# A fused scan and feed-forward kernel: 512 tokens a matmul instead of 256 from token 1024 on

## The chip, the cores and the metric

The kernel runs on one core of a Trainium2 chip. The metric is device time in microseconds; a lower number is better. A run's time is that of the core; "span" is the time from the first to the last instruction in the profiled execution.

## What is computed

```python
batch, n_heads, seq, head_dim, d_state = 4, 8, 768, 32, 16      # x, a, B, C
n_tokens, d_model, d_ff = 3072, 256, 2048                       # w_in, w_out

# a state-space scan, per batch and head (the reference goes in chunks of 32; any chunk gives the same)
L = exp(cum[i] - cum[j]) for i >= j, else 0          # cum: running sum of log(a) in the chunk
y = ((C @ B.T) * L) @ x + (C @ state) * exp(cum)
state = exp(sum(log a)) * state + B.T @ (x * exp(cum[-1] - cum))

# then a feed-forward layer on the 3072 tokens, 8 heads x 32 = 256 features
h = y @ w_in
g = h - tanh(h)
out = g @ w_out
```

All inputs are fp32 but the weights, which are fp64 and are converted on the chip into two fp32r parts (wh, wl).

## The kernel before

**Scan.** Each of the 4 sequences is cut into 7 chunks of 112 tokens (the last has 96), 28 chunks in all. A chunk has two parts on TensorE. `chunk_a` makes the decay exponents and C times B in one `att` tile (matmuls at L452 and L458); ScalarE takes the exponential (L462), VectorE multiplies (L466), GpSimd zeroes the upper triangle (L469). `chunk_y` makes y (L494) and the next state (L502) in a `y` tile in PSUM; ScalarE copies the state in four pieces to the next chunk's operand (L507) and y's high part to `xh` (L514), and VectorE subtracts to get the low part `xl` (L519). So the feed-forward input is held as two fp32r parts, high and low, one pair of tiles a sequence, two sequences at a time.

**Feed-forward.** The 2048 hidden features are 16 blocks of 128, taken in 8 pairs `u`. The tokens are 12 tiles `t` of 256. A step is one (t, u). `mm1` (L545) forms the hidden values of a tile and a pair of blocks in one PSUM bank `ph` (128 x 2 x 256): for each block, 6 matmuls of 256 columns (wh and wl with xh, wh with xl, each over two halves of the 256 features). `act` then does the tanh on ScalarE (L559), the subtraction on VectorE (L563), the high part `gh` on ScalarE (L567) and the low part `gl` on VectorE (L574). `mm2` (L595) adds the step's part of the output to one PSUM bank `po` (128 x 2 x 256): 12 matmuls of 256 columns. Each matmul has a weight load of its own.

PSUM: two banks `ph`, one `po`, one `y`, four for `att`.

**Order of the work.** The weights arrive and are converted (`load_w`, `conv`) while the first work runs, so the first four tiles (tokens 0 to 1023) go in four sweeps, each over two pairs `u`, and their output sums are kept in `pt` between sweeps (`keep`, L609 and L616). The eight tiles behind them go through all eight pairs at once. At its last pair a tile's sum is copied, on ScalarE and VectorE a half each (L629, L631; with `pt` added at L627 in the first four tiles), to `ob` and stored by two DMAs on SyncE's queue (`store`, L634). `mm2` is entered two steps (`LAG`) behind `mm1`. The chunks that a tile needs are spread over the steps of the tile ahead of it.

The order on each engine is not written by hand. Each operation is entered with its engine, a cost in us, what it reads and what it writes; `slot` names the buffers of a ring, and a buffer is free for its next use when the earlier readers are done. `Order.plan` simulates that list with priorities, in 16 rounds with random jitter and then 1500 random tries on the first 110 us, and keeps the best. The instructions are issued in the order of the simulated starts.

Of the kernel before, what the change touches and what calls it, by code (L numbers as in the profile page):

```python
# [31 lines left out]
NT = T // TT  # L32
# [12 lines left out]
SWEEPS = 0, 2, 4, 6, 8  # L45


class Order:
# [24 lines left out]
    def __call__(self, eng, cost, fn, r=(), w=(), dma=0, after=()):  # L73
# [134 lines left out]
def tile_ssm_moe(ctx: ExitStack, tc: tile.TileContext, a, x, bn, bc, wts, out):  # L208
# [16 lines left out]

    chunks, ends = {}, 0
    for t in range(NT):
        b, j = divmod(t, S // TT)
        end = b * CPB + -(-(j + 1) * TT // Q)
        chunks[t], ends = list(range(ends, end)), end  # L230
# [4 lines left out]
    SPAN = slice(len(chunks[0]), len(chunks[0]) + 7), slice(len(chunks[0]) + 7, NCK)  # L235
# [49 lines left out]
    wl = cp.tile([P, NCONV, 2, 2, 256], F32R, name="wl")  # L285

# [85 lines left out]
    def first_tile():  # L372
# [39 lines left out]
        for ck in range(len(chunks[0])):  # L412
# [65 lines left out]
    def chunk_y(ck):  # L478
# [4 lines left out]
        n_y = slot("y", 1)  # L483
# [6 lines left out]
        def fn():  # L490
            y = k["y"] = ps_y.tile([P, 2 * H * D], F32, tag="y", name=f"y{ck}")
# [17 lines left out]

        def fn_h():  # L510
            if c == 0:
                seq[b]["xh"] = p3.tile([P, 2, S], F32R, tag="xh", name=f"xh{b}", bufs=2)
            k["yv"] = k["y"][:, 0 : 2 * Q].rearrange("p (g q) -> p g q", g=2)[:, :, 0:q]
            nc.scalar.copy(seq[b]["xh"][:, :, c * Q : c * Q + q], k["yv"])  # L514

        def fn_l():
            if c == 0:
                seq[b]["xl"] = p3.tile([P, 2, S], F32R, tag="xl", name=f"xl{b}", bufs=2)
            nc.vector.tensor_tensor(out=seq[b]["xl"][:, :, c * Q : c * Q + q], in0=k["yv"],  # L519
                                    in1=seq[b]["xh"][:, :, c * Q : c * Q + q].bitcast(F32), op=ALU.subtract)  # L520
# [9 lines left out]
    def mm1(t, u):  # L530
        b, j = divmod(t, S // TT)
        d, ts = seq[b], slice(j * TT, (j + 1) * TT)
        cs = [c for c in range(CPB) if c * Q < ts.stop and (c + 1) * Q > ts.start]
        n_h, n_g = slot("ph", NPH), slot("g", 3)
        gs[t, u, 0] = [n_h, n_g]

        def fn():
            ph = ps_h.tile([P, 2, TT], F32, tag="ph", name=f"ph{t}_{u}")
            gs[t, u] = [ph]
            for j in range(2):  # L540

                for p in range(2):
                    for k in range(2):
                        for w_ in (wh, wl)[: 2 - p]:
                            nc.tensor.matmul(out=ph[:, j, :], lhsT=w_[:, u, 0, k, j * P : (j + 1) * P],  # L545
                                             rhs=d[("xh", "xl")[p]][:, k, ts], start=p == 0 and k == 0 and w_ is wh,
                                             stop=p == 1 and k == 1, skip_group_check=True)

        op("PE", 1.41, fn, r=[*[d["n_xh"][c] for c in cs], *[d["n_xl"][c] for c in cs], f"wh{u}.0", f"wl{u}.0"], w=[n_h])

    def act(t, u, eng):
        n_h, n_g = gs[t, u, 0]
        n_gh, n_gl = slot("gh", 3), slot("gl", 3)
        gs[t, u, 0] += [n_gh, n_gl]

        def fn_t():
            g = p3.tile([P, 2, TT], F32, tag="g", name=f"g{t}_{u}")
            gs[t, u].append(g)
            nc.scalar.activation(g, gs[t, u][0], AF.Tanh)  # L559

        def fn_s():
            ph, g = gs[t, u]
            nc.vector.tensor_tensor(out=g, in0=ph, in1=g, op=ALU.subtract)  # L563

        def fn_h():
            gh = p3.tile([P, 2, TT], F32R, tag="gh", name=f"gh{t}_{u}")
            nc.scalar.copy(gh, gs[t, u][1])  # L567
            gs[t, u].append(gh)

        def fn_l():  # L570
            _, g, gh = gs[t, u]
            gl = p3.tile([P, 2, TT], F32R, tag="gl", name=f"gl{t}_{u}")
            on = nc.vector if eng == "DVE" else nc.gpsimd
            on.tensor_tensor(out=gl, in0=g, in1=gh.bitcast(F32), op=ALU.subtract)  # L574
            gs[t, u].append(gl)
# [4 lines left out]
        op(eng, 0.8 if eng == "DVE" else 1.8, fn_l, r=[n_g, n_gh], w=[n_gl])  # L580

    def mm2(t, u, seg):

        _, _, n_h, n_l = gs[t, u, 0]
        if u == seg[0]:
            n_po[t, seg] = slot("po", 1)

        def fn():
            _, _, gh, gl = gs[t, u]
            if u == seg[0]:  # L590
                po[t, seg] = ps_o.tile([P, 2, TT], F32, tag="po", name=f"o{t}_{u}")
            for k, (w_, g) in enumerate(((wh, gh), (wl, gh), (wh, gl))):
                for j in range(2):
                    for e in range(2):
                        nc.tensor.matmul(out=po[t, seg][:, e, :], lhsT=w_[:, u, 1, j, e * P : (e + 1) * P],  # L595
                                         rhs=g[:, j, :], start=u == seg[0] and k == 0 and j == 0 and e == 0,
                                         stop=u == seg[-1] and k == 2 and j == 1, skip_group_check=True)

        op("PE", 1.41, fn, r=[n_h, n_l, f"wh{u}.1", f"wl{u}.1"], w=[n_po[t, seg]])
        if u == seg[-1]:  # L600
            if u < NCONV - 1:
                keep(t, seg)
            else:
                store(t, seg)

    def keep(t, seg):

        if seg[0]:
            op("DVE", 0.69, lambda: nc.vector.tensor_tensor(out=pts[t], in0=po[t, seg], in1=pts[t], op=ALU.add),  # L609
               r=[n_po[t, seg]], w=[n_pt[t]])  # L610
            return
        n_pt[t] = slot("pt", NSW)

        def fn():
            pts[t] = p1.tile([P, 2, TT], F32, tag="pt", name=f"pt{t}", bufs=NSW)
            nc.scalar.copy(pts[t], po[t, seg])  # L616

        op("ACT", 0.6, fn, r=[n_po[t, seg]], w=[n_pt[t]])

    def store(t, seg):  # L620
        name = op.pieces(slot("ob", 2), 2)

        def fn_c(i):
            if i == 0:
                obs[t] = p2.tile([P, 2, TT], F32, tag="ob", name=f"ob{t}")
            if t in pts:
                nc.vector.tensor_tensor(out=obs[t], in0=po[t, seg], in1=pts[t], op=ALU.add)  # L627
            elif i == 0:
                nc.scalar.copy(obs[t][:, 0], po[t, seg][:, 0])  # L629
            else:  # L630
                nc.vector.tensor_copy(out=obs[t][:, 1], in_=po[t, seg][:, 1])  # L631

        def fn_d(i):
            nc.sync.dma_start(out=out[i * P : (i + 1) * P, t * TT : (t + 1) * TT], in_=obs[t][:, i])  # L634

        if t < NSW:
            op("DVE", 0.69, lambda: fn_c(0), r=[n_po[t, seg], n_pt[t]], w=name)
        else:
            op("ACT", 0.36, lambda: fn_c(0), r=[n_po[t, seg]], w=[name[0]])
            op("DVE", 0.36, lambda: fn_c(1), r=[n_po[t, seg]], w=[name[1]])  # L640
        for i in range(2):
            op("SP", 0.42, lambda i=i: fn_d(i), r=[name[i]], dma=KB)
# [170 lines left out]
    for t in range(1, NT):  # L813
        g0, n = begin["t", t - 1], begin["t", t] - begin["t", t - 1]
        for i, ck in enumerate(chunks[t]):
            at_[ck] = g0 + i * n // len(chunks[t]), min(g0 + i * n // len(chunks[t]) + 1, g0 + n - 1)
# [63 lines left out]
```

## Time and profile before

| | us |
|---|---|
| Time, median of 3 runs (345.47 to 346.5) | 345.87 |
| Profiled execution: span | 344.3 |
| TensorE busy in the span | 330.2 (96%) |
| VectorE busy | 227.5 (66%) |
| ScalarE busy | 192.9 (56%) |
| GpSimd busy | 57.2 (17%) |

The profiled execution is a run by itself; its span is from its first to its last instruction, and no time of that execution beside the span is recorded. The median of the runs is 1.57 us above the span.

A line of a group reads: line of the kernel, engine, operation, out<-in with the names of the program's tiles, shape, count | busy us, mean ns of one | idle us of the engine just ahead of them, and what ended it. Matmuls overlap one another in the records (a matmul of 256 columns has a record of some 280 ns, and one starts every 110 to 120 ns), so the pace is read from the starts, or from the chain of work that ended last, which puts the pieces end to end. Some matmul records are missing. PE is TensorE's matmuls, PEld its weight loads, DVE VectorE, ACT ScalarE, POOL GpSimd, SP SyncE.

### The profile page before, as it was taken

To read this page: it belongs to the slowest core of one execution; us is meant where nothing else is said; L and a number is where in the kernel's file an instruction comes from. 1 tells how busy PE (TensorE), PEld (TensorE's weight loads), DVE (VectorE), ACT (ScalarE), POOL (GpSimd) and SP (SyncE) were. 2 spreads that over 40 slices of the span, in tenths; PEclk is the share of its full clock that TensorE was granted. 3 is DMA by queue.
4 is the path that set the end of the run, shared out by engine and by line. 5 is a ranking of instruction groups with operands and counts; after the bars stand their busy time and mean duration, and the time that the engine had idled before them with its cause. 6 is when DMAs were issued, how large, how long until landed. Compare 5 with 4: busy or idle time off the path is not lost.

```text
span 344.3 us, 8873 instructions
## 1 busy us (share of the span) xinstructions
PE 330.2 (96%) x3756; PEld 317.9 (92%) x3756; DVE 227.5 (66%) x339; ACT 192.9 (56%) x403; POOL 57.2 (17%) x69
## 2 busy tenths in 40 slices
PE   7939979999999999999999999999999999999995
PEld 6839879999999999999999999999999999999995
DVE  5996898999998875645654655555655555654552
ACT  7855977786554543534655646444554555554441
POOL 1544453340000110101211110210401110110000
PEclk9875989999999999999999999999999999999999
DMA  7929658614000011001211200200200100000100
GB/s 164 301 63 317 179 131 201 213 52 132 3 0 3 10 51 61 32 3 45 61 45 30 63 2 9 82 2 23 71 2 1 32 2 2 32 0 2 32 0 31
DMA packets 12471, 21.39 MB, mean 62 GB/s; under 512 B 2848, under 2 KB 7648, under 8 KB 12432
## 3 DMA queue, kind: packets, MB, share of 16 engines
q1 hardware_dynamic: 12432, 20.84, 21.4%
q8 instruction: 29, 0.48, 0.6%
q14 instruction: 10, 0.08, 0.1%
HBM read 17.51 MB, written 3.32 MB: 60 GB/s over the span
## 4 chain that ended last, share of the span: by engine, by line
PE 87%; DVE 3%; SPq 3%; DMA 3%; ACT 1%; issue 1%; POOL 0%; POOLq 0%; DVEq 0%; ACTq 0%
PE o L595 40%; PE ph L545 38%; PE y L494 3%; PE att L458 2%; DMA braw<-bn_d 2%; PE cp L381 1%; DMA bc<-bc_d 1%; PE att L452 1%; SPq L770 1%; SPq L278 1%; SPq L247 1%; PE y L502 1%; PE att L392 1%; DVE wm L310 0%; SPq L772 0%
## 5 line engine op out<-in xcount | busy, mean ns | idle before, releaser
L559 ACT ACTIVATE g<-ph 128x512 f32<-128x512 f32 x96 | 57.4, 598 | 91.5 <-PE ph L545 89.3
L563 DVE TENSOR_TENSOR g<-ph,g 128x512 f32<-128x512 f32 x96 | 65.9, 690 | 62.9 <-ACT g L559 62.9
L545 PE MATMUL ph<-xh,wh 128*128 128x256 f32 x384 | 101.3, 286 | 0.0
L545 PE MATMUL ph<-xh,wl 128*128 128x256 f32 x384 | 100.0, 283 | 0.0
L574 DVE TENSOR_TENSOR gl<-g,gh 128x512 fp32r<-128x512 f32 x96 | 67.0, 700 | 26.9 <-ACT gh L567 25.7
L545 PE MATMUL ph<-xl,wh 128*128 128x256 f32 x384 | 77.1, 282 | 0.0
L567 ACT CAST gh<-g 128x512 fp32r<-128x512 f32 x96 | 59.1, 619 | 28.7 <-DVE g L563 27.2
L545 PEld LDWEIGHTS ph<-xh,wh 128*128 128x128 f32 x384 | 73.8, 192 | 1.1 <-issue 0.4
L545 PEld LDWEIGHTS ph<-xh,wl 128*128 128x128 f32 x384 | 73.8, 192 | 0.0
L469 POOL TENSOR_SCALAR_AFFINE_SELECT lt<-lt 128x896 f32<-128x896 f32 (+1 forms) x25 | 34.0, 1359 | 203.9 <-DVE lt L466 203.9
L595 PE MATMUL o<-gh,wh 128*128 128x256 f32 x384 | 63.5, 287 | 0.0
L595 PE MATMUL o<-gl,wh 128*128 128x256 f32 x384 | 60.2, 278 | 0.0
L595 PE MATMUL o<-gh,wl 128*128 128x256 f32 x384 | 60.2, 278 | 0.0
L545 PEld LDWEIGHTS ph<-xl,wh 128*128 128x128 f32 x384 | 59.8, 192 | 0.0
L595 PEld LDWEIGHTS o<-gh,wh 128*128 128x128 f32 x384 | 51.2, 188 | 2.8
L595 PEld LDWEIGHTS o<-gl,wh 128*128 128x128 f32 x384 | 51.5, 188 | 0.0
L595 PEld LDWEIGHTS o<-gh,wl 128*128 128x128 f32 x384 | 51.5, 188 | 0.0
L466 DVE TENSOR_TENSOR lt<-att,lt 128x896 f32<-128x896 f32 (+1 forms) x25 | 26.7, 1067 | 6.8 <-ACT lt L462 6.8
L462 ACT ACTIVATE lt<-att 128x896 f32<-128x896 f32 (+1 forms) x25 | 22.6, 902 | 6.1 <-PE att L458 4.4
L507 ACT COPY x<-y 16x64 f32<-16x64 f32 x96 | 19.4, 202 | 8.6 <-DVE xl L519 7.1
L494 PE MATMUL y<-lt,x 128*32 128x112 f32 (+1 forms) x448 | 17.3, 274 | 5.4 <-POOL bc L352 3.3
L494 PEld LDWEIGHTS y<-lt,x 128*32 128x32 f32 x448 | 10.2, 113 | 9.2 <-POOL bc L352 3.4
(70 smaller groups left out, 232.8 us busy)
## 6 DMA issues: line engine op xcount, KB each, us to landing
raw<-w_d SPq DMA_DIRECT2D x16, 512.0 KB
x<-x_d SPq DMA_DIRECT2D x14, 256.0 KB
bc<-bc_d SPq DMA_DIRECT2D x56, 60.0 KB
out_d<-ob SPq DMA_DIRECT2D x24, 128.0 KB
braw<-bn_d SPq DMA_DIRECT2D x14, 112.0 KB
cum<-parts SPq DMA_DIRECT2D x1, 168.0 KB
rt_c<-cum SPq DMA_DIRECT2D x4, 27.0 KB
lt_c<-cum SPq DMA_DIRECT2D x4, 27.0 KB
```

The lines of the kernel that those rows point to most:

```text
L458: nc.tensor.matmul(out=at_[:, i, 2 + w, :], lhsT=bb[r, w], rhs=cc[r, w, 0:q], start=True, stop=True)
L462: nc.scalar.activation(k["l"][:, :, 0:q].rearrange("p (i w) q -> p i w q", i=4), k["a"][:, :, 0:2, :], AF.Exp)
L466: nc.vector.tensor_tensor(out=lt, in0=k["a"][:, :, 2:4, :], in1=lt, op=ALU.mult)
L469: nc.gpsimd.affine_select(out=k["l"][:, :, 0:q], in_=k["l"][:, :, 0:q], pattern=[[0, H], [1, q]], compare_op=ALU.is_ge, fill=0.0, base=N, ...
L494: nc.tensor.matmul(out=y[D * h : D * h + D, hg * Q : hg * Q + q], lhsT=d["x"][:, cg, P * hg + D * h : P * hg + D * h + D], rhs=k["l"][:, 4 ...
L507: nc.scalar.copy(grp[(ck + 1) // CPG]["x"][0:N, (ck + 1) % CPG, 2 * D * i : 2 * D * i + 2 * D], k["y"][D * i : D * i + N, H * D : H * D + ...
L545: nc.tensor.matmul(out=ph[:, j, :], lhsT=w_[:, u, 0, k, j * P : (j + 1) * P], rhs=d[("xh", "xl")[p]][:, k, ts], start=p == 0 and k == 0 an ...
L559: nc.scalar.activation(g, gs[t, u][0], AF.Tanh)
L563: nc.vector.tensor_tensor(out=g, in0=ph, in1=g, op=ALU.subtract)
L567: nc.scalar.copy(gh, gs[t, u][1])
L574: on.tensor_tensor(out=gl, in0=g, in1=gh.bitcast(F32), op=ALU.subtract)
L595: nc.tensor.matmul(out=po[t, seg][:, e, :], lhsT=w_[:, u, 1, j, e * P : (e + 1) * P], rhs=g[:, j, :], start=u == seg[0] and k == 0 and j = ...
```

## The change

- The tokens from 1024 on go in four tiles of 512 instead of eight of 256. A step is one tile and one block `f` of 128 features instead of a pair. `mm1` is 6 matmuls of 512 columns into one `ph` bank (128 x 1 x 512), `mm2` 6 matmuls of 512 columns.
- The output sum of such a tile is 128 x 512 for each half `e` of the output features: one half is in the `po` bank, the other in the bank that was `y`'s. Each half is copied by itself, 512 columns on ScalarE or VectorE, and stored by a DMA of 256 KB.
- The chunks that the first four tiles need (`early`, 0 to 9) still have their y in the `y` bank. Chunks 10 to 27 take a bank of the `ph` ring, which the first product uses too.
- `xh` and `xl` are one ring of two sequences each, since a tile of 512 tokens can span two sequences.
- The first four tiles of 256 tokens stay as they were in all four sweeps (`NARROW` is 4).
- A chunk is entered over the steps of the tile ahead, as before: chunks 10 to 13 are now spread over the 26 steps from the first step of narrow tile 3 on; before, chunks 12 and 13 were entered in the tile from 1024 on.
- `Order`: when a DMA writes a buffer that another DMA writes too, its issue now stays behind the other one's. The seed and the rounds are the same, the planner's entered cost of a piece of 512-column matmuls is 1.32.

```diff
 TT = 256
-NT = T // TT
+TW = 512
 SWEEPS = 0, 2, 4, 6, 8
+NARROW = 4
...
                 if dma and self.ops[j][0] == "DMA":
                     chain.add(j)
+                    soft.add(j - 1)
...
+    narrow = [(t * TT, TT) for t in range(NSW)]
+    wide = [(t * TW, TW) for t in range(T // TW)]
     chunks, ends = {}, 0
-    for t in range(NT):
...
+    for w in narrow + wide[NSW * TT // TW :]:
+        b, j = divmod(sum(w) - 1, S)
+        end = b * CPB + j // Q + 1
+        chunks[w], ends = list(range(ends, end)), end
...
+    early = range(next(iter(chunks[wide[NSW * TT // TW]])))
...
+    xh = cp.tile([P, 2, 2 * S], F32R, name="xh")
+    xl = cp.tile([P, 2, 2 * S], F32R, name="xl")
...
-        n_y = slot("y", 1)
+        n_y = slot("y", 1) if ck in early else slot("ph", NPH)
...
-            y = k["y"] = ps_y.tile([P, 2 * H * D], F32, tag="y", name=f"y{ck}")
+            pool, tag = (ps_y, "y") if ck in early else (ps_h, "ph")
+            y = k["y"] = pool.tile([P, 2 * H * D], F32, tag=tag, name=f"y{ck}")
...
+        at = b % 2 * S + c * Q
...
-            nc.scalar.copy(seq[b]["xh"][:, :, c * Q : c * Q + q], k["yv"])
+            nc.scalar.copy(xh[:, :, at : at + q], k["yv"])
...
-    def mm1(t, u):
+    def mm1(w, f):
+        at, n = w
...
+        u, ts = f // 2, slice(at % (2 * S), at % (2 * S) + n)
+        blocks = range(f % 2, f % 2 + TW // n)
         def fn():
-            ph = ps_h.tile([P, 2, TT], F32, tag="ph", name=f"ph{t}_{u}")
-            for j in range(2):
+            ph = ps_h.tile([P, TW // n, n], F32, tag="ph", name=f"ph{at}_{f}")
+            for j in blocks:
                 for p in range(2):
                     for k in range(2):
                         for w_ in (wh, wl)[: 2 - p]:
-                            nc.tensor.matmul(out=ph[:, j, :], lhsT=w_[:, u, 0, k, j * P : (j + 1) * P],
-                                             rhs=d[("xh", "xl")[p]][:, k, ts], ...
+                            nc.tensor.matmul(out=ph[:, j - f % 2, :], lhsT=w_[:, u, 0, k, j * P : (j + 1) * P],
+                                             rhs=(xh, xl)[p][:, k, ts], ...
...
-        if u == seg[0]:
-            n_po[t, seg] = slot("po", 1)
+        if f == seg[0]:
+            n_po[w, seg] = [slot("po", 1)] if n == TT else [slot("po", 1), slot("y", 1)]
...
             for k, (w_, g) in enumerate(((wh, gh), (wl, gh), (wh, gl))):
-                for j in range(2):
+                for j in blocks:
                     for e in range(2):
-                        nc.tensor.matmul(out=po[t, seg][:, e, :], lhsT=w_[:, u, 1, j, e * P : (e + 1) * P],
-                                         rhs=g[:, j, :], ...
+                        nc.tensor.matmul(out=po[w, seg][e], lhsT=w_[:, u, 1, j, e * P : (e + 1) * P],
+                                         rhs=g[:, j - f % 2, :], ...
...
-        op("PE", 1.41, fn, r=[n_h, n_l, f"wh{u}.1", f"wl{u}.1"], w=[n_po[t, seg]])
+        op("PE", 1.41 if n == TT else 1.32, fn, r=[n_h, n_l, f"wh{u}.1", f"wl{u}.1"], w=n_po[w, seg])
...
+        else:
+            for e in range(2):
+                op("DVE" if summed or e else "ACT", 0.69 if summed else 0.6, lambda e=e: fn_c(e),
+                   r=[n_po[w, seg][e], *used], w=[name[e]])
+        for e in range(2):
+            op("SP", 0.42, lambda e=e: fn_d(e), r=[name[e]], dma=KB * n // TT)
...
+    segs = []
+    for s, (i, j) in enumerate(zip(SWEEPS, SWEEPS[1:])):
+        for w in narrow if s < NARROW else wide[: NSW * TT // TW]:
+            segs.append((w, tuple(range(2 * i, 2 * j, TW // w[1]))))
+    segs += [(w, tuple(range(NF))) for w in wide[NSW * TT // TW :]]
```

More of the change, by code (lines that the diff above doesn't have):

```diff
@@ L233, in tile_ssm_moe @@
     KB = P * 1024
-    SPAN = slice(len(chunks[0]), len(chunks[0]) + 7), slice(len(chunks[0]) + 7, NCK)
+    early = range(next(iter(chunks[wide[NSW * TT // TW]])))
+    SPAN = slice(len(chunks[narrow[0]]), len(chunks[narrow[0]]) + 7), slice(len(chunks[narrow[0]]) + 7, NCK)
     def load_bc(G):
@@ L410, in fn_s @@
                                     fill=0.0, base=N, channel_multiplier=-1)
-        for ck in range(len(chunks[0])):
+        for ck in range(len(chunks[narrow[0]])):
             k = chs[ck]
@@ L508, in fn_c @@
                            k["y"][D * i : D * i + N, H * D : H * D + 2 * D])
+        at = b % 2 * S + c * Q
         def fn_h():
[L511 to L512 removed]
             k["yv"] = k["y"][:, 0 : 2 * Q].rearrange("p (g q) -> p g q", g=2)[:, :, 0:q]
[L514 removed]
+            nc.scalar.copy(xh[:, :, at : at + q], k["yv"])
         def fn_l():
[L517 to L520, printed above, removed]
+            nc.vector.tensor_tensor(out=xl[:, :, at : at + q], in0=k["yv"],
+                                    in1=xh[:, :, at : at + q].bitcast(F32), op=ALU.subtract)
         op("PE", 0.5 if last else 0.7, fn, r=[*k["n_l"], d["p_x"][cg], d["n_bw"]], w=[n_y])
@@ L527, in chunk_y @@
         op("DVE", 0.4, fn_l, r=[n_y, n_xh], w=[n_xl])
-    def mm1(t, u):
-        b, j = divmod(t, S // TT)
-        d, ts = seq[b], slice(j * TT, (j + 1) * TT)
-        cs = [c for c in range(CPB) if c * Q < ts.stop and (c + 1) * Q > ts.start]
+    def mm1(w, f):
+        at, n = w
+        cs = [(b, c) for b in range(NB) for c in range(CPB) if b * S + c * Q < at + n and b * S + min(c * Q + Q, S) > at]
         n_h, n_g = slot("ph", NPH), slot("g", 3)
-        gs[t, u, 0] = [n_h, n_g]
+        gs[w, f, 0] = [n_h, n_g]
+        u, ts = f // 2, slice(at % (2 * S), at % (2 * S) + n)
+        blocks = range(f % 2, f % 2 + TW // n)
         def fn():
-            ph = ps_h.tile([P, 2, TT], F32, tag="ph", name=f"ph{t}_{u}")
-            gs[t, u] = [ph]
-            for j in range(2):
+            ph = ps_h.tile([P, TW // n, n], F32, tag="ph", name=f"ph{at}_{f}")
+            gs[w, f] = [ph]
+            for j in blocks:
                 for p in range(2):
@@ L567, in fn_h @@
-            nc.scalar.copy(gh, gs[t, u][1])
-            gs[t, u].append(gh)
+            gh = p3.tile(shape, F32R, tag="gh", name=f"gh{w[0]}_{f}")
+            nc.scalar.copy(gh, gs[w, f][1])
+            gs[w, f].append(gh)
         def fn_l():
[L571 to L575, printed above, removed]
+            _, g, gh = gs[w, f]
@@ L577, in act @@
+            gl = p3.tile(shape, F32R, tag="gl", name=f"gl{w[0]}_{f}")
+            nc.vector.tensor_tensor(out=gl, in0=g, in1=gh.bitcast(F32), op=ALU.subtract)
+            gs[w, f].append(gl)
         op("ACT", 0.6, fn_t, r=[n_h], w=[n_g])
@@ L579, in act, with mm2 @@
         op("ACT", 0.62, fn_h, r=[n_g], w=[n_gh])
-        op(eng, 0.8 if eng == "DVE" else 1.8, fn_l, r=[n_g, n_gh], w=[n_gl])
-    def mm2(t, u, seg):
-        _, _, n_h, n_l = gs[t, u, 0]
-        if u == seg[0]:
-            n_po[t, seg] = slot("po", 1)
-        def fn():
-            _, _, gh, gl = gs[t, u]
-            if u == seg[0]:
-                po[t, seg] = ps_o.tile([P, 2, TT], F32, tag="po", name=f"o{t}_{u}")
+        op("DVE", 0.7, fn_l, r=[n_g, n_gh], w=[n_gl])
+    def mm2(w, f, seg):
+        at, n = w
+        _, _, n_h, n_l = gs[w, f, 0]
+        if f == seg[0]:
+            n_po[w, seg] = [slot("po", 1)] if n == TT else [slot("po", 1), slot("y", 1)]
+        u, blocks = f // 2, range(f % 2, f % 2 + TW // n)
+        def fn():
+            _, _, gh, gl = gs[w, f]
+            if f == seg[0]:
+                if n == TT:
+                    o = ps_o.tile([P, 2, TT], F32, tag="po", name=f"o{at}_{f}")
+                    po[w, seg] = o[:, 0], o[:, 1], o
+                else:
+                    po[w, seg] = (ps_o.tile([P, TW], F32, tag="po", name=f"o{at}_{f}"),
+                                  ps_y.tile([P, TW], F32, tag="y", name=f"oe{at}_{f}"))
@@ L599, in mm2 @@
-        op("PE", 1.41, fn, r=[n_h, n_l, f"wh{u}.1", f"wl{u}.1"], w=[n_po[t, seg]])
-        if u == seg[-1]:
+                        nc.tensor.matmul(out=po[w, seg][e], lhsT=w_[:, u, 1, j, e * P : (e + 1) * P],
+                                         rhs=g[:, j - f % 2, :],
+                                         start=f == seg[0] and k == 0 and j == blocks[0] and (n == TW or e == 0),
+                                         stop=f == seg[-1] and k == 2 and j == blocks[-1], skip_group_check=True)
@@ L601, in mm2, with partial, keep @@
+        op("PE", 1.41 if n == TT else 1.32, fn, r=[n_h, n_l, f"wh{u}.1", f"wl{u}.1"], w=n_po[w, seg])
+        if f == seg[-1]:
             if u < NCONV - 1:
-                keep(t, seg)
+                keep(w, seg)
             else:
-                store(t, seg)
-    def keep(t, seg):
+                store(w, seg)
+    def partial(w):
+        return pts[w[0] // TW][:, :, w[0] % TW : w[0] % TW + w[1]]
+    def keep(w, seg):
+        at, n = w
+        i = at // TW
+        if n == TW:
+            for e in range(2):
+                op("DVE", 0.69, lambda e=e: nc.vector.tensor_tensor(out=partial(w)[:, e], in0=po[w, seg][e], in1=partial(w)[:, e], op=ALU.add),
+                   r=[n_po[w, seg][e]], w=[n_pt[i, e, x] for x in range(2)])
+            return
+        half = at % TW // TT
@@ L608, in keep @@
         if seg[0]:
-            op("DVE", 0.69, lambda: nc.vector.tensor_tensor(out=pts[t], in0=po[t, seg], in1=pts[t], op=ALU.add),
-               r=[n_po[t, seg]], w=[n_pt[t]])
+            op("DVE", 0.69, lambda: nc.vector.tensor_tensor(out=partial(w), in0=po[w, seg][2], in1=partial(w), op=ALU.add),
+               r=n_po[w, seg], w=[n_pt[i, e, half] for e in range(2)])
             return
-        n_pt[t] = slot("pt", NSW)
+        if half == 0:
+            names = op.pieces(slot("pt", NSW * TT // TW), 4)
+            n_pt.update({(i, e, x): names[2 * e + x] for e in range(2) for x in range(2)})
@@ L614, in fn @@
         def fn():
[L615 to L629, printed above, removed]
-            else:
[L631 to L637, printed above, removed]
-        else:
[L639 to L642, printed above, removed]
+            if half == 0:
+                pts[i] = p1.tile([P, 2, TW], F32, tag="pt", name=f"pt{i}", bufs=NSW * TT // TW)
@@ new lines, in fn, with store, make, fn_c @@
+            nc.scalar.copy(partial(w), po[w, seg][2])
+        op("ACT", 0.6, fn, r=n_po[w, seg], w=[n_pt[i, e, half] for e in range(2)])
+    def store(w, seg):
+        at, n = w
+        summed = at < NSW * TT
+        used = [n_pt[at // TW, e, x] for e in range(2) for x in range(at % TW // TT, -(-(at % TW + n) // TT))] if summed else []
+        name = [slot("ob", 2)] * 2 if n == TT else [slot("ob", 2) for _ in range(2)]
+        def make(e):
+            obs[w, e] = p2.tile([P, TW // n, n], F32, tag="ob", name=f"ob{at}_{e}")
+            return obs[w, e]
+        def fn_c(e):
+            o = make(e)[:, 0]
+            if summed:
+                nc.vector.tensor_tensor(out=o, in0=po[w, seg][e], in1=partial(w)[:, e], op=ALU.add)
+            elif e == 0:
+                nc.scalar.copy(o, po[w, seg][0])
+            else:
+                nc.vector.tensor_copy(out=o, in_=po[w, seg][1])
+        def fn_b():
+            nc.vector.tensor_tensor(out=make(0), in0=po[w, seg][2], in1=partial(w), op=ALU.add)
+        def fn_d(e):
+            v = obs[w, 0][:, e] if n == TT else obs[w, e][:, 0]
+            nc.sync.dma_start(out=out[e * P : (e + 1) * P, at : at + n], in_=v)
+        if n == TT:
+            op("DVE", 0.69, fn_b, r=n_po[w, seg] + used, w=[name[0]])
+        else:
+            for e in range(2):
+                op("DVE" if summed or e else "ACT", 0.69 if summed else 0.6, lambda e=e: fn_c(e),
+                   r=[n_po[w, seg][e], *used], w=[name[e]])
+        for e in range(2):
+            op("SP", 0.42, lambda e=e: fn_d(e), r=[name[e]], dma=KB * n // TT)
@@ L793, in tile_ssm_moe @@
     conv(1)
-    segs = [(t, tuple(range(i, j))) for i, j in zip(SWEEPS, SWEEPS[1:]) for t in range(NSW)]
-    segs += [(t, tuple(range(NCONV))) for t in range(NSW, NT)]
-    steps = [(t, u, seg) for t, seg in segs for u in seg]
+    segs = []
[3 more added lines that the diff above has]
+    segs += [(w, tuple(range(NF))) for w in wide[NSW * TT // TW :]]
+    steps = [(w, f, seg) for w, seg in segs for f in seg]
     begin = {}
-    for g, (t, u, _) in enumerate(steps):
-        begin.setdefault(("t", t), g)
-        begin.setdefault(("u", u), g)
+    for g, (w, f, _) in enumerate(steps):
+        begin.setdefault(("t", w), g)
+        begin.setdefault(("u", f // 2), g)
     todo = {}
@@ L812, in tile_ssm_moe @@
     at_ = {}
[L813 to L816, printed above, removed]
+    ws = list(chunks)
+    for v, w in zip(ws, ws[1:]):
+        g0, n = begin["t", v], begin["t", w] - begin["t", v]
+        for i, ck in enumerate(chunks[w]):
+            at_[ck] = g0 + i * n // len(chunks[w]), min(g0 + i * n // len(chunks[w]) + 1, g0 + n - 1)
     for ck in at_:
@@ L824, in tile_ssm_moe @@
         if g < len(steps):
-            t, u, _ = steps[g]
-            mm1(t, u)
-            act(t, u, "DVE")
+            w, f, _ = steps[g]
+            mm1(w, f)
+            act(w, f)
             for fn, args in todo.get(g, ()):
```

26 lines of the change are left out of this document (11 added, 15 removed).

## The prediction

> **What bounds the kernel now.** I read the page's busy shares first, then stretches of time, then the waits of TensorE, then the chain that ended last. The page gives the span, TensorE's share, its busy tenths and the granted clock:
>
> ```profile
> span 344.3 us, 8873 instructions
> PE 330.2 (96%) x3756; PEld 317.9 (92%) x3756; DVE 227.5 (66%) x339; ACT 192.9 (56%) x403; POOL 57.2 (17%) x69
> PE   7939979999999999999999999999999999999995
> PEclk9875989999999999999999999999999999999999
> ```
>
> The times of the runs have a median of 345.87 us, 1.57 us above this span; I count differences in the span and apply them to the median. Stretches of time (busy us of PE, weight loads, DVE, ACT, POOL, then clock, DMA share, GB/s):
>
> ```profile
> 45.00:60.00 15.00, 13.25 (x224) 12.34 (x217) 12.96 (x19) 10.71 (x25) 6.45 (x7) 0.89 0.70 174
> 60.00:75.00 15.00, 15.00 (x206) 14.16 (x205) 14.64 (x19) 11.62 (x26) 6.00 (x7) 1.00 0.43 134
> 75.00:100.00 25.00, 25.00 (x223) 25.00 (x222) 23.43 (x34) 15.79 (x30) 1.18 (x1) 1.00 0.19 59
> 118.00:150.00 32.00, 32.00 (x315) 31.59 (x315) 19.07 (x29) 15.10 (x29) 2.56 (x3) 1.00 0.13 42
> 150.00:335.00 185.00, 185.00 (x2099) 178.97 (x2099) 102.85 (x153) 95.80 (x201) 21.72 (x22) 1.00 0.09 25
> ```
>
> From 60 us on TensorE has no gap and the full clock; VectorE is nearly full until 118 us and about 56% busy behind 150 us. TensorE's waits all lie ahead of 60 us; the longest are:
>
> ```profile
> PE y L494 <- POOL bc L352: 3.3, 1, 3.3
> PE att L452 <- DMA lt_c<-cum: 1.6, 1, 1.6
> PE att L452 <- DVE lt L466: 1.3, 3, 0.6
> ```
>
> So behind 60 us the time is TensorE's own work, and a change is worth what it does to the time of that work. The chain within 150 to 335 us, and two of the six groups of feed-forward matmuls there (the others have 234, 234, 228 and 228):
>
> ```profile
> by line: PE o L595 45.8%; PE ph L545 44.4%; PE y L494 4.1%; PE att L458 3.4%; PE att L452 1.6%; PE y L502 0.8%
> L545 PE MATMUL ph<-xh,wh 128*128 128x256 f32 x234 | 60.1, 280 | 0.0
> L595 PE MATMUL o<-gh,wh 128*128 128x256 f32 x229 | 38.7, 290 | 0.0
> ```
>
> Feed-forward is 90.2% of 185 us, 166.9 us for 1387 matmuls of 256 columns. Some of it is a toll behind each chunk of the scan, as the chain shows (start, us, what):
>
> ```profile
> 200.51 1.61 PE o L595 x12
> 202.12 1.41 PE ph L545 x12
> 203.53 1.41 PE o L595 x12
> 204.94 1.41 PE ph L545 x12
> 206.35 0.52 PE y L494 x16
> 206.88 0.12 PE y L502 x16
> 206.99 1.56 PE o L595 x12
> 208.55 1.36 PE ph L545 x12
> ```
>
> Twelve matmuls take 1.41 us after some chunk parts and 1.36 us after others, and the piece just behind a break 0.2 us more. The chain has 27 such breaks in this stretch (29 parts, two pairs adjacent): 5.4 us. (166.9 - 5.4) / 1387 = 116.4 ns a matmul. That is the number the change works on. How much of it is streaming of columns? At half clock the same matmuls can be timed (start us, us; nine starts lie between the two rows), with the clock of that stretch:
>
> ```profile
> 30.25 0.42 PE L545 MATMUL ph<-xh,wl 128*128 128x256 f32 x1
> 32.17 0.63 PE L545 MATMUL ph<-xl,wh 128*128 128x256 f32 x2
> 30.00:32.00 2.00, 2.00 (x10) 2.00 (x11) 1.84 (x3) 1.43 (x2) 0.08 (x1) 0.50 1.02 358
> ```
>
> 1.92 / 9 = 213.3 ns for 256 columns at clock 0.50. Half of it, 106.7 ns, is my estimate of pure streaming at clock 1.00, and 116.4 - 106.7 = 9.7 ns a matmul is excess that the half clock does not show (6.6 ns in the 1.36 us pieces, 11 ns in the 1.41 us pieces). Two matmuls of 256 pay it twice, one of 512 at most once.
>
> **The change part by part.**
>
> *Feed-forward of tokens 1024 to 3071.* Tokens 0 to 1023 keep their 256-token tiles in all four sweeps, so nothing changes there. Behind them 64 steps before and 64 after (8 tiles by 8 pairs of feature blocks; 4 tiles by 16 blocks). Each step has a piece of the first product and one of the second, so 128 pieces. A piece was 12 x 116.4 = 1.397 us and becomes 6 matmuls of 512 columns; 768 weight loads go. No row shows 512 columns at full clock. Bounds: with no excess, as at half clock, where a matmul also streams for 213.3 ns, a piece is 6 x 213.3 = 1.280 us and 128 x 0.117 = 15.0 us go. With the whole excess per matmul, 6 x 223.0 = 1.338 us, 7.6 us go. The bound below a gain is time that goes by columns alone: 6 x 232.8, nothing. I take 220 ns, the excess of the better pieces here: no full-clock piece shows less than 6.6 ns, and the half clock row says that longer streaming hides some. 6 x 220 = 1.320 us; 128 x 0.077 = **9.9 us off**. All of it is on the path, since PE has no gap.
>
> The Trainium skill, "TensorE: Matmul & The Clock Gate", section "Wait — 56ns, not 53.3ns?", has a start-to-start of columns over 2.4 GHz plus 2.5 ns. At 256 columns that would be 109.2 ns, where the trace has 116.4, so the trace does not agree there; at half clock it does (213.3). By the rule 512 columns take 215.8 ns, 1.295 us a piece, and the saving would be 13.1 us; it stands below as a rival. The same page's section "Back-to-back issue gap" has 131 ns a matmul at 512 columns in a stream with weight loads; that is below the streaming time seen here, and the trace speaks against it.
>
> *The element-wise work.* 512 elements a partition before and after, same count:
>
> ```profile
> L559 ACT ACTIVATE g<-ph 128x512 f32<-128x512 f32 x96 | 57.4, 598 | 91.5 <-PE ph L545 89.3
> L563 DVE TENSOR_TENSOR g<-ph,g 128x512 f32<-128x512 f32 x96 | 65.9, 690 | 62.9 <-ACT g L559 62.9
> L507 ACT COPY x<-y 16x64 f32<-16x64 f32 x96 | 19.4, 202 | 8.6 <-DVE xl L519 7.1
> L514 ACT CAST xh<-y 128x224 fp32r<-128x224 f32 x24 | 8.3, 346 | 1.7 <-PE y L502 1.3
> L519 DVE TENSOR_TENSOR xl<-y,xh 128x224 fp32r<-128x224 f32 x24 | 9.3, 389 | 5.0 <-ACT x L507 3.8 <-ACT xh L514 1.1
> L631 DVE COPY ob<-o 128x256 f32<-128x256 f32 x8 | 3.4, 423 | 5.4 <-ACT ob L629 5.4
> L627 DVE TENSOR_TENSOR ob<-o,pt 128x512 f32<-128x512 f32 x4 | 2.8, 692 | 0.3 <-PE o L595 0.2
> ```
>
> VectorE's 102.85 of 185 us becomes 102.85 of about 175: no new bound. Nothing.
>
> *y in the first product's banks (chunks 10 to 27).* A new wait. A bank of the first product is held from the matmuls' start to the end of the subtract: 1.32 + 0.60 + 0.69 us and some 0.3 us that I allow for hand-overs, about 2.9 us. A y holds it for 0.64 us on PE, four state copies of 0.202, one of 0.346 and the 0.389 subtract, about 2.3 us with hand-overs. Two banks offer 5.28 us per step of 2.64 us; a step needs 2.9 and, with 14 chunks in 48 steps, 0.7 more. So it fits at 68%, and the matmul that takes the bank after a y has a step's other product (1.32 us) and another first product (1.32 us) ahead of it, 2.64 against 2.3. Queued behind a waiting y or first product on PE is everything: the other product, whose inputs are ready, waits too. Bounds: nothing, and 0.7 us a chunk by 18 (12.6 us) if a y always blocks one bank while one 1.32 us piece is all the cover. I take **0.5 us**, near the first, since PE shows no wait with the same chain lengths. If the cover is thin, it is from 60 to 75 us, where VectorE (14.64 of 15) empties the banks late.
>
> *Chunks 12 and 13 move ahead of the last narrow sweep's end.* Their work is two parts on PE, which only change places, and about 1.5 us each on VectorE, with 12.9 us free from 118 to 150 us; their loads on SP's queue move with them, in a stretch with DMA share 0.13. Nothing.
>
> *Output sums in two banks, one in y's old bank.* Four tile ends instead of eight. Copies grow to 512 columns (0.60 on ACT as the tanh, 0.69 on DVE as L627), now side by side instead of one after the other as the 5.4 us of L631's wait show. Covered by the next first product, 1.32 us. Nothing.
>
> *x in a ring.* The same bytes at fixed places; the first write of sequence 2 needs the narrow tiles 0 to 2 to be done, which they are. Nothing.
>
> *The end.* The last copies and stores (timeline, then stretches):
>
> ```profile
> 340.80 0.37 ACT L629 COPY ob<-o 128x256 f32<-128x256 f32 x1 [3.56 <-PE o L595]
> 341.20 0.42 DVE L631 COPY ob<-o 128x256 f32<-128x256 f32 x1 [3.24 <-ACT ob L629]
> 342.00:342.50 0.50, 0.00 (x0) 0.00 (x0) 0.00 (x0) 0.00 (x0) 0.00 (x0) 1.00 0.79 260
> 342.50:343.00 0.50, 0.00 (x0) 0.00 (x0) 0.00 (x0) 0.00 (x0) 0.00 (x0) 1.00 0.78 264
> out_d<-ob SPq DMA_DIRECT2D x24, 128.0 KB
> ```
>
> Copies: 0.82 us in a row become 0.69, 0.1 off. Stores: 256 KB become 512 KB, at 262 GB/s 1.0 us more. **0.9 us on.** Bounds: 0.5 (the first store starts alone) and 1.5.
>
> *The order is planned anew.* The list of operations is another one, a DMA's issue now waits for the one before it on the same buffer, and the planner's random search ends elsewhere. This touches the ramp, the one place where PE waits. Its price either way is bounded by the longest of those waits, 3.3 us gone or paid once more. I take 0.
>
> Sum: -9.9 + 0.5 + 0.9 = -8.5 us; 345.87 - 8.5 = **337.4 us**.
>
> **The rivals.**
>
> *Excess hidden altogether.* A matmul that streams 213 ns hides what a 107 ns one can't; the half clock row speaks for it, the absence of any full-clock piece without excess against it. At 215.8 ns (the rule cited above): 13.1 us off, 345.87 - 13.1 + 1.4 = 334.2; at 213.3, 332.3. Chance 0.25.
>
> *The ramp comes out worse, or y costs some time, while the gain stands:* 3 to 5 us lost, 340.5 to 342.5. Chance 0.10.
>
> *The first product's banks become the bound (slower).* With y in one of two banks, PE stands before the next first product until the y is emptied: 2.3 + 0.2 us, against 1.32 + 0.5 of cover, 0.7 us a chunk. 18 chunks: 12.6 us, 345.87 - 9.0 + 12.1 = about 349. It decides from 9.0 / 18 = 0.5 us a chunk on. For it: no spare bank is left, ACT does five copies for each y. Against it: 68% by the sum above, and PE without a wait now. Chance 0.10.
>
> *The change does not do what it says:* time goes by columns (232.8 ns for 512). Then 345.87 + 1.4 = 347.3. Against it stands the half clock row. Chance 0.05.
>
> **How the numbers follow.** My own case, excess of 6 to 10 ns, has 0.50; with the bounds of its terms it goes from 335.5 to 341. A difference under 0.3% (1 us) can't be told from none. The range reaches from the first rival's lower end (332.3) to the second's upper end (342.5), rounded outwards, and leaves out the two slower cases: 332 to 343. Faster 0.84 (the first two rivals and my own, less 0.01), same 0.03, slower 0.13.
>
> **What the profile of the changed kernel would show.** Right: pieces of six in 1.30 to 1.35 us on the chain behind 150 us; no row of PE waiting for the first product's banks (releaser the subtract, or a y's last subtract); 512 KB after the last copy, about 2 us of DMA; PE's start of gapless work at 60 us give or take 3. Wrong: idle of PE in front of y or first-product matmuls behind 60 us; six matmuls in 1.39 us; a longer ramp.

## The result and the profile after

The changed kernel takes 349.36 us (median of 4 runs, 348.95 to 349.47), the kernel before 345.67. The ratio is 1.0128, 95% interval 1.0091 to 1.0164: slower by 1.3%, where 337.4 us was forecast.

The page of the changed kernel, then its stretches of time (columns as in the prediction):

```profile
span 347.7 us, 7300 instructions
PE 334.1 (96%) x2988; PEld 283.6 (82%) x2988; DVE 226.5 (65%) x335; ACT 193.2 (56%) x399; POOL 54.1 (16%) x69
```
```profile
60.00:75.00 15.00, 14.55 (x201) 13.82 (x191) 14.96 (x20) 13.74 (x27) 5.03 (x5) 1.00 0.71 211
75.00:100.00 25.00, 25.00 (x250) 24.59 (x249) 21.35 (x31) 15.22 (x28) 2.45 (x3) 1.00 0.09 27
150.00:335.00 185.00, 185.00 (x1339) 145.85 (x1338) 101.17 (x150) 95.17 (x193) 19.46 (x21) 1.00 0.07 22
```

768 weight loads and matmuls are gone, and weight loads are busy for 79% instead of 97% of the late stretch. TensorE still has no gap there. So the work itself did not get shorter. The chain (the work that ended last, end to end) shows it, first in the sweeps (narrow pieces), then in the tiles of 512 tokens:

```profile
93.75 2.88 PE ph L553 x24
96.63 2.83 PE o L611 x24
...
310.45 1.39 PE ph L553 x6
311.84 0.23 PE o L611
...
313.22 1.39 PE ph L553 x6
```

Six matmuls of 512 columns take 1.39 us in the first product; the second product's six fill the 1.38 us from 311.84 to 313.22. That is 230 to 231 ns a matmul, 115 to 116 per 256 columns, against 116.4 before. And the narrow pieces of the sweeps, which the change leaves as they were, went from 1.36 or 1.41 us to 1.44 (first product) and 1.42. The same sweeps in the chain of the kernel before, at each of its two paces:

```profile
93.85 2.72 PE o L595 x24
96.57 2.72 PE ph L545 x24
...
120.58 1.41 PE ph L545 x12
121.99 1.41 PE o L595 x12
```

The feed-forward is 2304 units of 256 columns (a matmul of 512 is two). The table has the start of a unit in TensorE's matmul records. Up to about unit 192 lies the ramp, where weights and inputs still arrive and TensorE has gaps; about unit 768 the tokens from 1024 on begin.

| us at | before | after | after, ring 64 bytes up | the same, seed 24 and cost 1.39 |
|---|---|---|---|---|
| unit 192 | 68.6 | 71.0 | 68.9 | 64.8 |
| unit 768 | 137.3 | 144.2 | 140.7 | 136.1 |
| end of span | 344.3 | 347.7 | 344.2 | 339.7 |

The change lost 2.4 us in the ramp. From unit 192 to 768 it lost 4.5 us: about 2.3 are chunk parts that moved ahead (three y and three att there, one y and two att before, with the 0.2 us that the piece behind each break loses), and the rest, 2.2, are the slower narrow pieces. Behind unit 768 it won 3.5 us to the end of the span. The moved chunk parts are about 2.3 of these and the 512 columns 1.5 (64 pieces of each product at 1.386 and 1.385 us, the mean between chunk parts, where the prediction has 1.397 for before); the end takes 0.5 back.

### The profile page after: what moved, and what is told of

The parts are those of the page before. It is cut to its first block, busy times and chain, and to the rows that moved or that the text cites. A ratio compares the mean times of both kernels' runs of the same rounds, so it can differ in the third digit from the quotient of the medians.

```text
span 347.7 us, 7300 instructions
## 1 busy us (share of the span) xinstructions
PE 334.1 (96%) x2988; PEld 283.6 (82%) x2988; DVE 226.5 (65%) x335; ACT 193.2 (56%) x399; POOL 54.1 (16%) x69
## 4 chain that ended last, share of the span: by engine, by line
PE 85%; DMA 7%; SPq 2%; DVE 2%; ACT 1%; issue 1%; POOL 1%; ACTq 0%
PE ph L553 39%; PE o L611 25%; PE oe L611 13%; PE y L502 3%; PE att L465 3%; DMA raw<-w_d 2%; DMA bc<-bc_d 2%; DMA x<-x_d 2%; DMA braw<-bn_d 1%; PE att L459 1%; SPq L252 1%; PE y L510 1%; DVE lt L473 1%; SPq L283 1%; SPq L273 1%
## 5 line engine op out<-in xcount | busy, mean ns | idle before, releaser
L553 PE MATMUL ph<-xh,wh 128*128 128x256 f32 (+1 forms) x256 | 88.4, 355 | 1.2 <-ACT xh L522 0.9
L553 PE MATMUL ph<-xh,wl 128*128 128x256 f32 (+1 forms) x256 | 85.7, 344 | 0.0
L553 PE MATMUL ph<-xl,wh 128*128 128x256 f32 (+1 forms) x256 | 66.8, 343 | 0.0
L553 PEld LDWEIGHTS ph<-xh,wh 128*128 128x128 f32 x256 | 49.9, 195 | 7.9 <-ACT xh L522 1.0
L553 PEld LDWEIGHTS ph<-xh,wl 128*128 128x128 f32 x256 | 50.1, 196 | 4.9
L611 PE MATMUL o<-gh,wh 128*128 128x256 f32 (+1 forms) x192 | 48.3, 333 | 0.2
L611 PE MATMUL o<-gh,wl 128*128 128x256 f32 (+1 forms) x192 | 45.8, 320 | 0.0
L611 PE MATMUL o<-gl,wh 128*128 128x256 f32 (+1 forms) x192 | 45.5, 318 | 0.0
L611 PE MATMUL oe<-gh,wh 128*128 128x512 f32 x64 | 25.3, 395 | 0.0
L611 PE MATMUL oe<-gh,wl 128*128 128x512 f32 x64 | 25.2, 394 | 0.0
```

Of the source, the lines that this page charges most:

```text
L553: nc.tensor.matmul(out=ph[:, j - f % 2, :], lhsT=w_[:, u, 0, k, j * P : (j + 1) * P], rhs=(xh, xl)[p][:, k, ts], start=p == 0 and k == 0 a ...
L611: nc.tensor.matmul(out=po[w, seg][e], lhsT=w_[:, u, 1, j, e * P : (e + 1) * P], rhs=g[:, j - f % 2, :], start=f == seg[0] and k == 0 and j ...
```

## The experiments

The theory to test has two halves. An fp32r matmul's time goes by its columns, in wide matmuls as in narrow ones; and the losses come from the place of x in SBUF (the on-chip memory that the operands are read from) and from the ramp. The rivals: the excess is per matmul or per weight load and something else eats the gain; the change itself lengthens the ramp.

**Pace of single matmuls.** A kernel with blocks of matmuls alone (no scan, no feed-forward): `block(name, N, n)` issues n matmuls of N columns, each with its weight load, into one bank.

> No scan and no feed-forward, only blocks of fp32r and bf16 matmuls with weight loads, each block with one thing changed; its time says nothing. Read is the start-to-start time in each block. Theory, time goes by columns: at full clock 256 columns take 113 to 118 ns and 512 take 226 to 232 ns in every fp32r block, the same with one weight block for all, and the 128-column block takes 57 to 59. Rival, the excess is per matmul or per weight load: 512 take 220 to 224 ns, and the excess moves when the weights stay the same. Within the theory: if the four bytes of an operand are the limit, bf16 blocks take 107 to 109 and 213 to 216; if it is the array's real clock, bf16 takes 113 to 118 and 226 to 232 too; if it is current, the zero blocks are faster than the others; if it is other engines' traffic, the blocks under busy VectorE and ScalarE are slower than those without.

Its timeline (start us, us, what); the time of a block is the distance to the next start:

```profile
18.26 8.80 PE L76 MATMUL a<-xr 128*128 128x256 f32 x72
26.90 8.35 PE L76 MATMUL b<-xr 128*128 128x512 f32 x36
35.09 10.83 PE L76 MATMUL c<-xr 128*128 128x128 f32 x96
45.76 4.41 PE L76 MATMUL d<-xr 128*128 128x256 f32 x35
...
147.15 21.16 PE L76 MATMUL bf<-xb 128*128 128x256 bf16 x204
168.25 0.40 PE L86 MATMUL by<-xs 128*32 128x112 f32 x8
```

fp32r: 8.64 / 72 = 120.0 ns at 256 columns, 8.19 / 36 = 227.5 at 512, 10.67 / 96 = 111.1 at 128. The same weights throughout, zeros as data, another bank each time, no accumulation, VectorE and ScalarE busy beside it: each such pair of blocks (72 of 256 and 36 of 512) took 16.8 to 16.9 us, as these two (16.83). So the data, the bank, accumulation and the other engines are out. With the moving operand 64 bytes on the pair took 16.73 us, 117.8 and 229.2 ns. The bf16 row is 72 matmuls of 256, 36 of 512 and 96 of 128 columns in 21.1 us; by their starts they take 109.3, 215.8 and 56.8 ns. The Trainium skill ("TensorE: Matmul & The Clock Gate", section "Wait — 56ns, not 53.3ns?") gives 21.0 us for the row: the rule holds for bf16 and fails for fp32r. The expectation was wrong in two points: 256 columns take 120.0 ns here, above its 113 to 118, and 128 columns take 111 ns, not 57 to 59.

**Place.** The same kernel with the moving operand started elsewhere, `rhs=src[:, off + N*i : ...]`.

> No scan and no feed-forward, only blocks of fp32r matmuls with weight loads; its time says nothing. Each pair of blocks (256 columns, 512 columns) reads its moving operand from another start in SBUF: 0 to 128 bytes on in steps of 8 or 16 bytes, a second copy 128 KB further up (64 bytes off a multiple of 128 at its start, on it with 16 elements more), weights moved by 64 bytes, and behind parts shaped like y and att. Theory, the start of the moving operand within 128 bytes sets the pace: 256 columns take 120 ns on a multiple of 128 bytes and 113 to 118 at 64 bytes more, in both copies, the far copy the other way round by its number; 512 columns 227 to 232 in each. Rival, the distance from the weights: the far copy is faster in all its blocks, and the shift does nothing. If an excess per matmul is hidden by longer streaming, 512 columns come to 216 to 220 at some start.

```profile
23.04 5.92 PE L71 MATMUL low_a_n<-mv,xr 128*128 128x256 f32 x48
28.80 5.63 PE L71 MATMUL low_a_w<-mv,xr 128*128 128x512 f32 x24
34.26 5.92 PE L71 MATMUL low_b_n<-mv,xr 128*128 128x256 f32 x48
...
79.29 5.60 PE L71 MATMUL low_f_n<-mv,xr 128*128 128x256 f32 x48
84.73 5.66 PE L71 MATMUL low_f_w<-mv,xr 128*128 128x512 f32 x24
90.22 5.91 PE L71 MATMUL low_g_n<-mv,xr 128*128 128x256 f32 x48
```

At the weights' place within 128 bytes (a) 256 columns take 120.0 ns and 512 take 227.5; 64 bytes off (f) they take 113.3 and 228.8. At the eight other starts 256 took 114 to 120 and 512 took 230 to 233.3. The copy 128 KB up gave 113.8 where it lay 64 bytes off and 119.8 where it did not, so distance is out. Moving the weights by 64 bytes instead gave 117.7, moving both 119.8: it is the difference of the two that counts. No start brought 512 columns below 227.5. Behind parts shaped like y and att the usual step at 64 bytes off was 118 ns instead of 113.3, so the same place has two paces. The run ends with blocks of 128 and of 64 columns, each with its load of 128 weight columns, and with the clock of the last two:

```profile
231.66 5.47 PE L71 MATMUL short_a_s<-mv,xr 128*128 128x128 f32 x48
236.97 7.12 PE L71 MATMUL shorter_a_t<-mv,xr 128*128 128x64 f32 x48
243.90 10.48 PE L71 MATMUL short_b_s<-mv,xr 128*128 128x128 f32 x48
254.18 10.39 PE L71 MATMUL shorter_b_t<-mv,xr 128*128 128x64 f32 x48
244.00:254.00 10.00, 10.00 (x49) 10.00 (x48) 0.00 (x0) 0.00 (x0) 0.00 (x0) 0.50 0.01 2
254.00:264.00 10.00, 10.00 (x49) 10.00 (x48) 0.00 (x0) 0.00 (x0) 0.00 (x0) 0.50 0.00 0
```

At full clock a step takes 111 ns with 128 columns and 111 to 112 with 64 (up to 240.5 us, where the clock falls), so below some 111 ns the columns no longer set the pace, and the fp32r weight load is the likely floor. At clock 0.50 both take 213 to 214 ns, as long as the 256 columns of the prediction's half-clock row. That row therefore did not time the streaming of 256 columns alone: it is also the floor of that clock, with weight loads busy for all of its 2.00 us.

**Fewer weight columns.** `lhsT=xr[:, P*i : P*i + M]` with M = 128, 64, 32.

> No scan and no feed-forward, only blocks of fp32r matmuls with weight loads; its time says nothing. Weights of 128, 64 and 32 columns, 256 and 512 moving columns, the moving operand at the weights' place within 128 bytes or 64 bytes off it. Theory, the excess comes with the loading of fp32r weights beside the stream: with 32 weight columns 256 moving columns come under 111 ns and 512 under 219, and the place no longer matters. Rival, it lies in the fp32r stream itself: 113 to 120 and 227 to 233 ns at any number of weight columns. The fine steps of 4 bytes look for a start better than 113.3 ns.

```profile
24.45 5.92 PE L71 MATMUL cols_a_same_n<-mv,xr 128*128 128x256 f32 x48
30.21 5.63 PE L71 MATMUL cols_a_same_w<-mv,xr 128*128 128x512 f32 x24
35.68 5.82 PE L71 MATMUL cols_a_shift_n<-mv,xr 128*128 128x256 f32 x48
...
68.73 5.62 PE L71 MATMUL cols_c_same_n<-mv,xr 128*32 128x256 f32 x48
74.18 5.71 PE L71 MATMUL cols_c_same_w<-mv,xr 128*32 128x512 f32 x24
79.73 5.61 PE L71 MATMUL cols_c_shift_n<-mv,xr 128*32 128x256 f32 x48
85.18 5.71 PE L71 MATMUL cols_c_shift_w<-mv,xr 128*32 128x512 f32 x24
```

With 32 weight columns 256 moving columns take 5.45 / 48 = 113.5 ns at both places and 512 take 231; with 64, 113.5 and 228 to 230. So two things make the excess over the 106.7 ns of the prediction (bf16 gives nearly the same for 256 more columns, 215.8 - 109.3 = 106.5). One, 6.8 ns per 256 columns, stays however short the weight load is: it belongs to the fp32r stream and at least doubles with its length (228 to 231 ns at 512). The other, 6.5 ns at the weights' own place, comes with a full load of 128 weight columns at 256 moving columns, depends on the place, and is gone with a shorter load. The theory that the load makes all of it fell. The place is not all that sets the second part: at 64 bytes off one block of this run took 117.9 ns and a later one, with the same operands, 113.3. The fine steps of 4 bytes found no start better than 113.3, and went up to 122.3 at 256 columns.

**The ring alone, and the ring 64 bytes up.** The kernel before with `xh` and `xl` as the change has them; then with one line ahead of them (and one behind, so that nothing else changes its place within 128 bytes). The order on every engine is that of before in both.

```diff
+    xh = cp.tile([P, 2, 2 * S], F32R, name="xh")
+    xl = cp.tile([P, 2, 2 * S], F32R, name="xl")
```
```diff
+    cp.tile([P, 16], F32, name="pad0")
     xh = cp.tile([P, 2, 2 * S], F32R, name="xh")
```

> The kernel before with x in the ring of the change and nothing else; the order on every engine is that of before. Theory, place in SBUF sets the pace of the narrow first product: its pieces take 1.42 to 1.44 us as in the sweeps of the changed kernel, over 96 steps 3 to 6 us, 349 to 352. Rival, the pace there comes from the order of the work: 345.7, pieces of 1.36 and 1.41.

> The kernel before with x in the ring, the ring moved up by 64 bytes. Theory, the start within 128 bytes: pieces of 1.36 and 1.41 us again, 344 to 346.5. Rival, the region of SBUF or the ring's longer rows: 350 to 354 as with the ring alone.

The ring alone is slower: ratio 1.0203 (1.0131 to 1.0275), median 352.6 us. Moved up by 64 bytes it is level with before: 1.0021 (0.9991 to 1.0051). Both medians lie just above what was expected (349 to 352, 344 to 346.5). The chains, the ring alone first, the moved ring behind it:

```profile
207.81 1.42 PE o L595 x12
209.23 1.44 PE ph L545 x12
```
```profile
204.01 1.41 PE ph L547 x12
205.42 1.37 PE o L597 x12
```

The places are worked out from the sizes of the tiles, no trace has addresses: the weights wh lie on a multiple of 128 bytes in all of these; before, xh and xl lay 64 bytes off one; in the ring they lie on one; moved, 64 bytes off again. The theory of the place holds, and region and row length are out. Not all of it is explained. The second product reads neither xh nor xl, and its operands keep their places, yet it takes 1.42 us a piece with the ring alone, and 1.37 or 1.41 with the ring moved. In the kernel before both products change together between 1.36 and 1.41 us (113.3 and 117.5 ns a matmul) at the chunk parts, much like the two paces of the blocks at 64 bytes off. What picks one of the two was not found.

**The changed kernel with its ring moved.**

> The changed kernel with its ring moved up by 64 bytes. Theory, the start within 128 bytes: the narrow first-product pieces of the sweeps go from 1.44 to 1.36 or 1.41, some 2 us; the wide ones change by under 1%, so 346 to 348. Rival, region or rows: 349 within 1 us.

346.68 us, ratio to before 1.0043 (1.0011 to 1.0075): 2.7 us better than the change as it was, and within what was expected. The narrow first-product pieces of the sweeps are back at 1.41 us, the second product's at 1.37:

```profile
91.17 2.83 PE ph L555 x24
94.00 2.73 PE o L613 x24
```

By the table the sweeps (unit 192 to 768) give 1.4 of these, 71.8 us instead of 73.2. The rest lies in the ramp, where the clock differs too: 0.975 over the profiled run, 0.965 in that of the change as it was.

**The ramp.** The seed of the planner's search, in the changed kernel and in the one before (there with the change's rule for DMA issues, which alone leaves the order of before as it was).

> The changed kernel with seed 1 in the planner's random search. Theory, the ramp is a draw: the 192nd matmul (in units of 256 columns) is reached 1 to 4 us away from the changed kernel's 71.0 us and the time moves by the same, 346 to 353. Rival, the change itself makes the ramp longer: 349 within 1 us.

> The kernel before with seed 1 and with the changed kernel's order of DMA issues (which alone leaves the order of before as it was). Theory, the ramp is a draw and the seed of before a good one: 346.5 to 350. Rival, the ramp does not depend on the draw: 345.7 within 1 us.

With seed 1 the changed kernel takes 345.35 us, ratio to before 1.0001 (0.9977 to 1.0025): 4 us better by the draw alone, unit 192 at 67.0 instead of 71.0 us. (346 to 353 us had been expected.) The kernel before with seed 1 can't be told from its own seed: 1.0028 (0.9989 to 1.0067); that its own was a good one, as expected, is not shown. So the ramp is a draw for the changed kernel, and its own seed has the worst of the ramps that were run. The clock granted there goes with it (changed kernel, kernel before, then seed 24 of below):

```profile
30.00:40.00 10.00, 10.00 (x139) 9.06 (x138) 7.51 (x10) 6.66 (x13) 4.99 (x5) 0.65 0.36 104
```
```profile
30.00:40.00 10.00, 9.77 (x165) 8.94 (x169) 7.44 (x12) 7.49 (x18) 4.35 (x6) 0.78 0.69 197
```
```profile
30.00:40.00 10.00, 9.43 (x180) 8.42 (x183) 8.09 (x12) 8.04 (x20) 4.47 (x5) 0.89 0.60 145
```

The runs of one and the same kernel show what this is worth: before took 343.2 to 344.7 us where its mean clock was 0.985 and 346.0 to 346.7 where it was 0.970. The changed kernel's four runs were all at 0.964 or 0.965. Why its order keeps the clock low longer was not tried.

**Place and draw together, and a better version.** The ring 64 bytes up with seed 1; the same with a planner's cost of 1.39 for a wide piece (what it takes) and seed 24; and two controls.

```diff
-        op("PE", 1.41 if n == TT else 1.32, fn,
+        op("PE", 1.41 if n == TT else 1.39, fn,
```

> The changed kernel with the ring 64 bytes up and seed 1. Theory, place and ramp are separate losses and their gains add: from 349.4, 2 to 2.7 us by the place and about 4 by the draw, so 342.5 to 344, below before. Rival, both act on the same ramp: 345 to 346.

> As before it, with the planner's cost of a wide piece set to the measured 1.39 and seed 24, whose planned end is the earliest of 25 seeds (336.3 us, where the changed kernel's seed has 338.9 and the kernel before 339.0). Theory, the order planned with true costs is followed: 342 to 344. Rival, the half clock at the start, which the plan does not know, decides: anywhere from 343 to 349.

> The kernel before with the best of 25 seeds by the planned end (338.6 us against 339.0), and with the changed kernel's order of DMA issues. Theory, the gain of seed 24 belongs to the wide kernel's list of operations, whose planned ends lie at 336.3 to 339.0, while those of the kernel before lie at 338.6 to 340.4: 344 to 346, no gain. Rival, any kernel gains 3 us from a searched seed: 341 to 343.

> The changed kernel with the ring 64 bytes up and the planner's cost of a wide piece at the measured 1.39, with its own seed. Theory, the seed makes the gain of seed 24 and the cost little: 346 to 348, as with the ring moved alone (346.7). Rival, the true cost makes the order: 342 to 344.

With seed 1, 344.4 us, ratio 0.9974 (0.9946 to 1.0002): the gains did not quite add (342.5 to 344 was expected), and it can't be told from before. With seed 24, **341.41 us, ratio 0.9885 (0.9843 to 0.9928)**: faster than both kernels, 0.6 us below the expected range. Of the 4.6 us of span that it wins on before, 3.8 lie in the ramp. The true cost with the change's own seed is no better than the moved ring without it: 1.0047 (1.0015 to 1.0079). So the cost alone does not make the gain; seed 24 with the old cost was not run. The best planned seed for the kernel before gives 1.0028 (0.9984 to 1.0072), no gain that can be measured; its times spread from 343.6 to 350.2 us, and their median, 347.95, lies above the 344 to 346 that was expected. Two other seeds of the narrow kernel thus did not give the gain. Whether another one would was not tried.

## Why the prediction was wrong

**The step that failed is the price of a 512-column matmul.** It took 220 ns and a gain of 9.9 us; measured are 230 to 231 ns in the kernel, which is 1.5 us, and about 227 at best in any block. The prediction worked out an excess of 9.7 ns a matmul at full clock, saw none at half clock, and read this as "longer streaming hides some". That reading does not stand: at half clock 64, 128 and 256 columns all take 213 to 214 ns, so the row shows a floor that does not move with the columns up to 256, and nothing of what a longer stream would hide. At full clock most of the excess goes with the columns: with short weight loads 256 columns take 113.5 ns and 512 take 228 to 231, some 0.44 to 0.45 ns a column. That this part belongs to the fp32r stream, and not to the matmuls or the loads, is shown by the blocks; why the stream runs at that rate is open. The price was in the text, as a rival with 0.05 ("time goes by columns", 347.3 us); the two losses below make most of the rest. Of the signs that the prediction named for being wrong two came in full, six matmuls in 1.39 us and a longer ramp, and the third, idle time ahead of a first product, with 0.3 us.

**x in a ring, priced at nothing, was wrong.** With the ring the narrow pieces of the sweeps cost 2.2 us in the changed kernel, 1.4 of which the 64 bytes won back; the ring alone costs the kernel before 2.4 us between the same units, and 2% in all. The prediction looked at bytes and waits of the new tile and not at where it lands.

**The order planned anew, priced at 0 and within 3.3 us either way,** measured 2.4 us, inside its bounds. But the bounds were too narrow for the draw: seed 1 alone moved the time by 4 us. The prediction counted the waits and left out the clock, which differs with the order (0.65 to 0.89 in the stretch from 30 to 40 us).

**y in the first product's banks** was right: 0.5 us taken, and TensorE's only waits ahead of a first product in the whole run are

```profile
PE ph L553 <- ACT xh L522: 0.9, 1, 0.9
PE ph L553 <- DVE g L573: 0.3, 1, 0.3
```

Of these the second alone, at 68 us, waits for a bank. In the stretch from 60 to 75 us VectorE is busy for 14.96 of 15 us, as the prediction said of the place where the cover is thin. So the rival that was to make it slower is not what did. (Its sum takes off 0.5 us that the 9.0 does not hold: 345.87 - 9.0 + 12.6 is 349.5, not 349. That this is near the measured time is chance.) **Two sums, eight copies less, element-wise work**: nothing, as predicted. **The end**: 0.9 us taken, 0.5 measured (from the last matmul's end to the end of the span 4.0 us against 3.6), since the larger stores ran faster, where the prediction had 262 GB/s:

```profile
345.00:345.50 0.50, 0.00 (x0) 0.00 (x0) 0.00 (x0) 0.00 (x0) 0.00 (x0) 1.00 1.02 381
345.50:346.00 0.50, 0.00 (x0) 0.00 (x0) 0.00 (x0) 0.00 (x0) 0.00 (x0) 1.00 1.04 389
```

The rule of the Trainium skill that was weighed there ("TensorE: Matmul & The Clock Gate", section "Wait — 56ns, not 53.3ns?"; 215.8 ns at 512 columns) was further off than the value taken, 220 ns, where fp32r took 230 to 231.

## What to carry to other kernels

Before paying for wider matmuls, find out whether the excess over pure streaming is per matmul or per column; a row at another clock could not tell them apart here, and a row of another width in the same data type can. When a tile is laid out anew, price its place in SBUF against the operand that is read beside it: 64 bytes were worth 2% here. And when an order is made by a random search, compare two changes over several draws, or the draw is what is measured.

## What the runs showed of the hardware

- fp32r at full clock, 128 weight columns, blocks without breaks (runs pace, place, cols): 113.3 to 122.3 ns for 256 columns, 226.7 to 236.5 for 512, 111 for 128 and for 64. bf16 took 109.3, 215.8 and 56.8 ns for 256, 512 and 128.
- At clock 0.50, fp32r matmuls of 64 and 128 columns (run place) and of 256 (kernel before) all took 213 to 214 ns.
- The pace at 256 columns depends on the moving operand's start against the weights' within 128 bytes: 120 ns at the same place and 113.3 to 117.9 at 64 bytes off; at 512 columns 227.4 to 228.4 and 228.7 to 233.3.
- In run place the granted clock fell to 0.50 in the middle of matmuls of 64 columns without a gap: a step took 111 to 112 ns up to 240.5 us and 213 to 215 behind.
- Stores of 128 x 512 fp32 went at 381 to 389 GB/s, stores of 128 x 256 at 260 to 264.
